# Where the identity, ones and minus-one tiles lie in SBUF, in a fused attention, mixture and gating kernel

## The chip, the cores and the metric

The kernel runs on one core of one Trainium2 chip. The metric is device time in microseconds (us) of one execution; lower is better. The number compared is the median of the runs.

## The reference, cut to what matters

```python
def reference(q, k, v, moe..., moe2...):
    attn = softmax(q k^T / 8 - slope_h * |i - j|, causal, window 128) @ v   # 4 x 8 heads x 576 x 64
    x = attn as [4, 576, 512]
    xn = (x - mean) / sqrt(var + 1e-6) * g_ln
    x = x + relu(xn @ w_ch1) @ w_ch2                                       # 512 -> 2048 -> 512
    h = gelu(x @ w_in); u, v = halves of h                                  # 512 -> 1024
    v = w_sg @ layernorm(v) * g + b_sg
    return x + (u * v) @ w_out
```

The weights arrive as 64-bit floats in pairs of 32-bit words, and every large product is made of three: high times high, low times high and high times low, in the 32-bit matmul type that takes one pass.

## The kernel before

Phase 1 (`phase1`) computes the attention and the first feed-forward layer together. Phase 2 (`Phase2`) computes the gated layer. The feed-forward layer is cut into nine groups of 256 tokens (`g` 0 to 8) and eight slices of the hidden width (`j` 0 to 7); a step of `m1` (line 835) or `m2` (line 846) is two halves of 12 matmuls each. Each matmul loads a stationary block of 128 x 128 from the weight tiles and streams a moving block of 128 x 256 past it. In the profile the moving operand's name stands first behind the arrow and the stationary one's second.

Between these steps a list scheduler (`Sched`, `Op`), whose clock is made of durations written by hand, puts the attention's pieces and the norm's pieces on TensorE. For this case four of them matter, since they are what interrupts the stream of steps:

- the transposes, line 606: `pe.transpose(..., e.t, ident)`. The probabilities are stationary, the identity tile is the moving operand. They are the last piece of every attention burst (score products, line 466, value products, line 650, then two or four transposes), and the next feed-forward matmul follows them;
- the token sums for the mean, line 703: the moving operand is the tile of sums, the ones tile is stationary;
- the sums of squares, line 751: the squares are stationary, one column of ones is moving;
- the broadcast of the reciprocal roots, line 761: the root is stationary, the identity tile is moving.

The tile of minus one is used twice only: for the first two pieces of weights (`NLO = 2`) the low half is made on TensorE (lines 368 and 369), as identity times the weight minus the rounded weight.

The tiles of constants lie in one pool at the bottom of SBUF (`body`, pool `cst`): identity, minus and ones of 512 bytes a partition each, then two small ones. In the built program they start at the bytes 1152, 1664 and 2176 of a partition, which is 128 mod 256 for all three. Everything that is allocated on the left behind them follows from 2752, which is 192 mod 256: `hh`, `hl`, `xh` and `xl` of groups 1 to 8 (the moving operands of the steps) start at 192 mod 256, the weight tiles `w1` and `w2` at 0 mod 256. The `xh` and `xl` of group 0 come from the pool `ap2` on the other side, at 224 mod 256. The tiles of probabilities (`t`) are at 224 mod 256 as well. In phase 2 all tiles are allocated from the right.

The reciprocal roots (`rstd`) lie in a ring of three buffers of 1024 bytes. A tile of zeros for the first, warming matmuls is the first tile that this ring hands out; the roots of groups 0, 1, 2 and so on follow.

Of the kernel before, what the change touches and what calls it, by code (L numbers as in the profile page):

```python
# [7 lines left out]
F32 = mybir.dt.float32  # L8
F32R = mybir.dt.float32r
U8 = mybir.dt.uint8  # L10
I32 = mybir.dt.int32
ACTF = mybir.ActivationFunctionType
# [220 lines left out]
def phase1(tc, nc, a, x2d, cst, p2):  # L233

    sync, act, dve, pool, pe = nc.sync, nc.scalar, nc.vector, nc.gpsimd, nc.tensor
    ident, minus, ones, g1, mh, far = cst
    sched = Sched()

    hp = tc.alloc_tile_pool(name="hp", bufs=2)
# [1 line left out]
    cp = tc.alloc_tile_pool(name="cp", bufs=2)  # L241
    np_ = tc.alloc_tile_pool(name="np", bufs=1)
# [21 lines left out]
    P = {}  # L264
# [11 lines left out]
    def by(o):  # L276

        return {"DVE": dve, "POOL": pool}[o.eng]
# [25 lines left out]
    start, first = {}, {}  # L304
# [14 lines left out]
    def place(n):  # L319

        if n < 24:
            return n // 8, n % 8, slice(0, 512)
        m = n - 24
        z, c0 = (m % 4, m // 4) if m < 8 else (m // 2, m % 2)
        return 3, z, slice(256 * c0, 256 * c0 + 256)
# [14 lines left out]
    def weights(n):  # L340
        q, z, c = place(n)
        w = c.stop - c.start
        late = n >= 24
        st, sc = ("st", NS) if late else ("big", NB), ("sc", NC) if late else ("sc0", 3)
        pri = (WPRI[n] if n < 24 else need[n] - WBACK) + n / 100
        yield Op("SP", 500, WEARLY.get(n, pri), need=["split"] if late else [], slots=[st + (("b3", n),)],
                 token=("wl", n), size=1024 * w)
        p = P["st"] if late else big
        s = p.tile([128, w], I64, tag="st", name="st", bufs=st[1])
        sync.dma_start(out=s, in_=(a["w1"][q, z] if z < 4 else a["w2"][q, z - 4])[:, c])  # L350
        yield Op("ACT", 90 + .93 * w, pri, need=[("wl", n)], slots=[sc + (("w", n),)])
        j = Split64(nc, p, sc[1], s)
        j.first()
        yield Op("DVE", 75 + .51 * w, pri, port=True)
        j.bits(0)
        yield Op("DVE", 75 + .51 * w, pri, port=True)
        j.bits(1)
        yield Op("DVE", 64 + 1.05 * w, pri, port=True)
        j.bits(2)
        yield Op("DVE", 64 + 1.05 * w, pri, token=("b3", n), port=True)  # L360
        j.bits(3)
        yield Op("ACT", 110 + .82 * w, pri, need=["quarter"] if late else [])
        h, l = ((w1 if z < 4 else w2)[q][y][:, z % 4, c] for y in range(2))
        act.activation(out=h, in_=j.x, func=ACTF.Copy)
        if n < NLO:
            yield Op("PE", 1080, pri, need=["cst"], slots=[("h", 2, ("w", n))])
            ps = ps_h.tile([128, 2, 256], F32, tag="h", name="ps_w").rearrange("p a b -> p (a b)")
            pe.matmul(ps, ident, j.x, start=True, stop=False)
            pe.matmul(ps, minus, h, start=False, stop=True)
            yield Op("ACT", 490, pri, token=("w", n))  # L370
            act.activation(out=l, in_=ps, func=ACTF.Copy)
            return
        o = Op(None, 0, pri, token=("w", n), alt=[("POOL", 150 + 2.15 * w, 0), ("DVE", 64 + 1.05 * w, DVEX, 1)])
        yield o
        by(o).tensor_tensor(out=l, in0=j.x, in1=h.bitcast(F32), op=ALU.subtract)
# [300 lines left out]
    xhl, rstd = {}, {}  # L676

    def ln_tile(name):
        return np_.tile([128, 2, 256], F32, tag="ls", name=name, bufs=2)
# [170 lines left out]
    def constants():  # L850
        yield Op("SP", 500, CSTP, token="cst0", size=6 * 2 ** 15, slots=[("ls", 2, "al2")])
        t = ln_tile("cst").rearrange("p a b -> p (a b)").bitcast(BF16)[:, 0:768].rearrange("p (n c) -> p n c", n=6)
        sync.dma_start(out=t, in_=a["cst"].rearrange("p (n c) -> p n c", n=6))
        for z in sms:
            pool.memset(z, 1e-9)
        dve.memset(both, 0.0)
        sched.free["DVE"] = 2300
        yield Op("DVE", 320, -1000, need=["cst0"], token="msk")
        dve.tensor_copy(mask[:, 0:2], t[:, 3:5])
        dve.tensor_scalar(mask[:, 2], t[:, 3], -1.0, 1.0, ALU.mult, ALU.add)  # L860
        yield Op("ACT", 550, -1000, need=["cst0"], token="cst")
        act.activation(out=ident, in_=t[:, 0], func=ACTF.Copy)
        act.activation(out=minus, in_=t[:, 0], func=ACTF.Copy, scale=-1.0)
        for x0 in range(0, 8, 2):
            yield Op("DVE", 270, -1000, need=["cst0"], token="al" if x0 == 6 else None)
            for x in (x0, x0 + 1):
                dve.tensor_scalar(dist[:, x], t[:, 1], 2.0 ** (2 - x), None, ALU.mult)
        yield Op("DVE", 270, -62, token="unf")
        dve.tensor_copy(munf[:, 0], t[:, 5])
        dve.tensor_scalar(munf[:, 1], t[:, 5], -1.0, 1.0, ALU.mult, ALU.add)  # L870
        yield Op("SP", 500, -960, size=2 ** 11)
        sync.dma_start(out=g1, in_=a["g1"])
        for x in range(8, 12):
            yield Op("ACT", 200, -30)
            act.activation(out=dist[:, x], in_=t[:, 2], func=ACTF.Copy, scale=2.0 ** (2 - 4 * ((x - 8) // 2) - x % 2))
        yield Op(None, 0, 0, token="al2")
# [35 lines left out]
    for gen in ([warm(), constants()] + [load_wide(slice(x, y), t) for x, y, t in LW]  # L912
                + [moe(), open_split(), last_quarter(), end_attention()]
                + [weights(n) for n in range(40)] + [norm(g) for g in range(G)]
                + [load(s) for s in runs if not s.wide] + [scores(s) for s in runs] + [burst(s) for s in runs if s.n >= KB] + [unit(e) for e in units]):
        sched.spawn(gen)
# [372 lines left out]
def body(tc, nc, a):  # L1289
    sync, act, dve, pool, pe = nc.sync, nc.scalar, nc.vector, nc.gpsimd, nc.tensor  # L1290
    dp = tc.alloc_tile_pool(name="dp", bufs=1, space=DRAM)
    x2d = [dp.tile([128, 4, 256], F32, name="x2d%d" % g) for g in range(G)]
    with tc.manual_schedule(), tc.tile_pool(name="cst", bufs=1) as cp:
        ident = cp.tile([128, 128], F32, name="ident")
        minus = cp.tile([128, 128], F32R, name="minus")
        ones = cp.tile([128, 128], F32, name="ones")
        g1 = cp.tile([128, 4], F32, name="g1")
        mh = cp.tile([128, 2], F32, name="mh")
        mh, far = mh[:, 0:1], mh[:, 1:2]
        pool.memset(mh, -0.5)  # L1300
        pool.memset(far, NEG)
        pool.memset(ones, 1.0 / DM)
        p2 = Phase2(tc, nc, a, x2d, mh)
        phase1(tc, nc, a, x2d, (ident, minus, ones, g1, mh, far), p2)


def wsT(w):
# [45 lines left out]
```

## Time and profile before

| what | value |
|---|---|
| median of 3 runs | 738.98 us (738.39 to 739.26) |
| profiled execution, its own time | 738.73 us |
| its span, first to last instruction | 737.0 us |
| TensorE busy with matmuls | 720.1 us, 98% of the span |
| VectorE, ScalarE, GpSimd busy | 460.3, 309.1 and 249.2 us |
| mean granted clock of TensorE | 0.993 |

The profile gives busy times by engine and by line, the chain of work that ended last, followed back from the end, and for a stretch of time the busy time and the granted clock. Busy time of matmuls counts overlapping instructions once; so a busy TensorE says nothing of how densely the matmuls follow each other. That is read from the chain: a piece of it that holds 24 matmuls of one line gives, divided by 24, the time from one start to the next (the pitch).

### The profile page before, as it was taken

To read this page: it belongs to the slowest core of one execution; us is meant where nothing else is said; L and a number is where in the kernel's file an instruction comes from. 1 tells how busy PE (TensorE), PEld (TensorE's weight loads), DVE (VectorE), ACT (ScalarE), POOL (GpSimd) and SP (SyncE) were. 2 spreads that over 40 slices of the span, in tenths; PEclk is the share of its full clock that TensorE was granted. 3 is DMA by queue.
4 is the path that set the end of the run, shared out by engine and by line. 5 is a ranking of instruction groups with operands and counts; after the bars stand their busy time and mean duration, and the time that the engine had idled before them with its cause. 6 is when DMAs were issued, how large, how long until landed. Compare 5 with 4: busy or idle time off the path is not lost.

```text
span 737.0 us, 16770 instructions
## 1 busy us (share of the span) xinstructions
PE 720.1 (98%) x6714; PEld 691.0 (94%) x6714; DVE 460.3 (62%) x1200; ACT 309.1 (42%) x795; POOL 249.2 (34%) x296
## 2 busy tenths in 40 slices
PE   6889999999999999999999999999999999999997
PEld 3569999999999999999999999999999999999997
DVE  6999989899572643644543537636676647647632
ACT  5887664554342422522423524323454233344410
POOL 1445250333421321411313324124747307326320
PEclk8999999999999999999999999999999999999999
DMA  8564532023221110111112323403330150160002
GB/s 307 161 213 131 174 118 72 28 93 95 66 98 29 56 51 24 48 59 58 27 49 59 84 85 141 146 29 123 103 116 1 49 159 1 60 198 1 1 33 97
DMA packets 51629, 63.48 MB, mean 86 GB/s; under 512 B 10336, under 2 KB 38880, under 8 KB 51552
## 3 DMA queue, kind: packets, MB, share of 16 engines
q1 hardware_dynamic: 51552, 62.41, 26.5%
q8 instruction: 53, 0.87, 0.5%
q14 instruction: 24, 0.20, 0.1%
HBM read 52.96 MB, written 9.44 MB: 85 GB/s over the span
## 4 chain that ended last, share of the span: by engine, by line
PE 83%; DVE 7%; ACT 5%; issue 2%; POOL 1%; DMA 1%; SPq 0%; DVEq 0%; ACTq 0%
PE ps_h L835 24%; PE acc L846 24%; PE ps_s L1196 8%; PE ps_o L1223 7%; PE ps_v L1100 5%; PE ps_u L1180 5%; PE s L466 2%; PE tps L606 1%; PE o L650 1%; ACT t L517 1%; PE o L606 1%; DVE sc L94 1%; DMA bb<-in_bsg 1%; PE tps L650 1%; DVE sc L97 1%
## 5 line engine op out<-in xcount | busy, mean ns | idle before, releaser
L776 DVE SCALAR_TENSOR_TENSOR hl<-ps_h,hh 128x512 fp32r<-128x512 f32 x72 | 49.7, 690 | 106.6 <-ACT hh L774 105.8
L846 PE MATMUL acc<-hh,w2h 128*128 128x256 f32 x576 | 93.6, 285 | 0.0
L835 PE MATMUL ps_h<-xh,w1h 128*128 128x256 f32 x576 | 92.1, 282 | 0.0
L774 ACT ACTIVATE hh<-ps_h 128x512 fp32r<-128x512 f32 x72 | 42.8, 595 | 116.7 <-PE ps_h L835 116.0
L846 PE MATMUL acc<-hl,w2h 128*128 128x256 f32 x576 | 89.7, 278 | 0.3 <-DVE hl L776 0.3
L835 PE MATMUL ps_h<-xh,w1l 128*128 128x256 f32 x576 | 89.7, 278 | 0.0
L835 PE MATMUL ps_h<-xl,w1h 128*128 128x256 f32 x576 | 89.7, 278 | 0.0
L846 PE MATMUL acc<-hh,w2l 128*128 128x256 f32 x576 | 89.6, 278 | 0.0
L475 POOL TENSOR_SCALAR_AFFINE_SELECT m<-m 128x256 f32<-128x256 f32 (+1 forms) x87 | 41.7, 481 | 136.6 <-ACT m L555 121.8
L835 PEld LDWEIGHTS ps_h<-xh,w1h 128*128 128x128 f32 x576 | 77.2, 189 | 1.3 <-issue 1.2
L846 PEld LDWEIGHTS acc<-hh,w2h 128*128 128x128 f32 x576 | 77.5, 189 | 0.3
L846 PEld LDWEIGHTS acc<-hl,w2h 128*128 128x128 f32 x576 | 76.7, 188 | 0.5 <-DVE hl L776 0.5
L835 PEld LDWEIGHTS ps_h<-xh,w1l 128*128 128x128 f32 x576 | 76.8, 188 | 0.0
L835 PEld LDWEIGHTS ps_h<-xl,w1h 128*128 128x128 f32 x576 | 76.8, 188 | 0.0
L846 PEld LDWEIGHTS acc<-hh,w2l 128*128 128x128 f32 x576 | 76.8, 188 | 0.0
L517 ACT ACTIVATE t<-t,sm 128x128 f32<-128x128 f32 x144 | 56.3, 392 | 28.0 <-DVE sm L511 27.8
L525 POOL TENSOR_TENSOR t<-t,sm 128x256 f32<-128x256 f32 x46 | 28.8, 626 | 72.4 <-DVE sm L521 38.7
L1090 POOL TENSOR_TENSOR gl<-gt,gh 128x576 fp32r<-128x576 f32 x16 | 23.4, 1461 | 49.3 <-ACT gh L1089 46.0
L590 ACT ACTIVATE x<-o 128x256 f32<-128x256 f32 (+1 forms) x40 | 14.3, 358 | 58.3 <-PE o L606 46.1
L85 ACT ACTIVATE sc<-st 128x512 f32<-128x512 f32 (+1 forms) x52 | 30.6, 597 | 16.3 <-DMA st<-in_w 6.6
L1134 ACT ACTIVATE ge<-ge 128x512 f32<-128x512 f32 (+1 forms) x34 | 22.4, 658 | 35.6 <-DVE ge L1133 35.6
L97 DVE SCALAR_TENSOR_TENSOR sc<-st,sc 128x512 int32<-128x512 int32 (+1 forms) x52 | 34.9, 678 | 0.1
(168 smaller groups left out, 1631.9 us busy)
## 6 DMA issues: line engine op xcount, KB each, us to landing
st<-in_w SPq DMA_DIRECT2D x24, 512.0 KB, 4.2
x2d<-x SPq DMA_DIRECT2D x18, 256.0 KB, 2.0
out<-xr SPq DMA_DIRECT2D x15, 288.0 KB, 2.1
st<-in_w SPq DMA_DIRECT2D x16, 256.0 KB, 2.6
st<-in_wi SPq DMA_DIRECT2D x8, 512.0 KB, 3.8
st<-x2d SPq DMA_DIRECT2D x8, 512.0 KB, 4.9
xr<-x2d SPq DMA_DIRECT2D x8, 512.0 KB, 6.6
rq<-in_q SPq DMA_DIRECT2D x28, 128.0 KB, 2.8
```

The costliest lines, as they stand in the source:

```text
L85: self.nc.scalar.activation(out=self.x, in_=self.wh.bitcast(F32), func=ACTF.Abs)
L97: dve.scalar_tensor_tensor(out=xi, in0=self.wl, scalar=29, in1=xi, op0=ALU.logical_shift_right, op1=ALU.bitwise_or)
L475: pool.affine_select(out=out, in_=in_, pattern=pat, compare_op=ALU.is_ge, fill=0.0, base=-1 if up else 0, channel_multiplier=1 if up else -1)
L517: act.activation(out=t[:, h], in_=t[:, h], func=ACTF.Exp, bias=st[:, h:h + 1], scale=-1.0, accum_out=sums[:, h, 0:1])
L774: act.activation(out=h, in_=ps, func=ACTF.Relu)
L776: dve.scalar_tensor_tensor(out=l, in0=ps, scalar=0.0, in1=h.bitcast(F32), op0=ALU.max, op1=ALU.subtract)
L835: pe.matmul(ps[:, half], w[:, kc, f], m[:, kc], start=kc == 0 and x == 0, stop=kc == 3 and x == 2)
L846: pe.matmul(accs[half][:, d], w[:, f, ds], m[:, k], start=fi and d == 0 and k == 0 and x == 0, stop=la and k == 1 and x == 2, skip_group_c ...
L1100: self.nc.tensor.matmul(ps[:, cs], xs[s][:, kc, c0:c0 + 128], self.wv[m][:, kc, cs], start=kc == 0 and x == 0 and z == 0, stop=kc == 3 and ...
L1180: pe.matmul(ps[:, c], wu[s][:, kc, ds], self.x[m][:, kc, c], start=kc == 0 and x == 0, stop=kc == 3 and x == 2)
L1196: pe.matmul(ps[:, c], l, r[:, c], start=n == 0, stop=n == len(mm) - 1)
L1223: pe.matmul(ps[:, c], wo[s][:, kc, ds], gated[b][m][:, kc, c], start=n == 0, stop=n == 11)
```

## The change

The pool of constants begins with an unused tile of 192 bytes (`gap`) and ends with one of 64 bytes (`end`). The identity and ones tiles start at 1344 and 1856, which is 64 mod 256. The tile of minus one leaves the pool; it takes the second buffer of the ring of the roots (`rstd`), whose tiles start at 192 mod 256. The pool is 256 bytes smaller than before, so that what is allocated behind it moves down by 256 bytes and keeps its place mod 256. No instruction of an engine is added or taken away in the source, and the scheduler's durations are the same.

```diff
-    ident, minus, ones, g1, mh, far = cst
+    ident, ones, g1, mh, far = cst
...
             pe.matmul(ps, ident, j.x, start=True, stop=False)
-            pe.matmul(ps, minus, h, start=False, stop=True)
+            pe.matmul(ps, P["minus"], h, start=False, stop=True)
...
         act.activation(out=ident, in_=t[:, 0], func=ACTF.Copy)
-        act.activation(out=minus, in_=t[:, 0], func=ACTF.Copy, scale=-1.0)
+        P["minus"] = np_.tile([128, 256], F32, tag="rstd", name="minus", bufs=3).bitcast(F32R)[:, 0:128]
+        act.activation(out=P["minus"], in_=t[:, 0], func=ACTF.Copy, scale=-1.0)
...
     with tc.manual_schedule(), tc.tile_pool(name="cst", bufs=1) as cp:
+        cp.tile([128, 192], U8, name="gap")
         ident = cp.tile([128, 128], F32, name="ident")
-        minus = cp.tile([128, 128], F32R, name="minus")
         ones = cp.tile([128, 128], F32, name="ones")
         g1 = cp.tile([128, 4], F32, name="g1")
         mh = cp.tile([128, 2], F32, name="mh")
         mh, far = mh[:, 0:1], mh[:, 1:2]
+        cp.tile([128, 64], U8, name="end")
...
-        phase1(tc, nc, a, x2d, (ident, minus, ones, g1, mh, far), p2)
+        phase1(tc, nc, a, x2d, (ident, ones, g1, mh, far), p2)
```

## Rows read from the trace of the kernel before

**Rows 1.** Stretches: window, length, busy us (instructions) by engine, TensorE clock, DMA.
```profile
49.00:52.40 3.40, 3.40 (x29) 2.15 (x19) 3.40 (x9) 2.41 (x8) 0.31 (x2) 0.50 0.60 216
...
60.00:210.00 150.00, 149.32 (x1466) 144.18 (x1466) 129.44 (x356) 82.01 (x225) 53.49 (x68) 1.00 0.31 96
210.00:464.00 254.00, 254.00 (x2689) 248.21 (x2686) 123.28 (x392) 87.88 (x269) 64.76 (x101) 1.00 0.20 60
```

**Rows 2.** Chain that ended last, 244 to 283 us: start, length, what.
```profile
244.58 0.43 PE ps_ln L703 x2
245.01 2.83 PE acc L846 x24
...
255.55 0.34 PE ps_ln L751 x4
255.89 2.93 PE ps_h L835 x24
258.83 0.44 PE ps_r L761 x4
259.27 2.73 PE acc L846 x24
262.00 2.72 PE ps_h L835 x24
...
267.92 0.22 PE tps L606 x2
268.14 1.39 PE acc L846 x12
269.52 2.72 PE ps_h L835 x24
...
280.78 0.22 PE tps L606 x2
281.00 1.42 PE acc L846 x12
282.42 2.83 PE ps_h L835 x24
```

**Rows 3.** The same view, 130 to 141 us: group 0's first products among others.
```profile
130.33 2.74 PE acc L846 x24
133.07 2.83 PE ps_h L835 x24
135.91 2.75 PE acc L846 x24
138.66 2.83 PE ps_h L835 x24
```

**Rows 4.** TensorE's groups by form: line, out<-moving,stationary, shapes, count, busy, mean ns, idle.
```profile
L606 PE MATMUL tps<-ident,t 128*128 128x128 f32 x98 | 21.3, 297 | 6.9 <-POOL t L525 4.8 <-ACT t L481 1.7 <-ACT m L555 0.2
L606 PE MATMUL o<-ident,t 128*128 128x128 f32 x46 | 10.1, 301 | 0.0
L751 PE MATMUL ps_ln<-ones,sq 128*128 128x1 f32 x60 | 7.3, 239 | 0.0
L761 PE MATMUL ps_r<-ident,var 128*128 128x128 f32 x36 | 5.7, 280 | 0.4 <-POOL var L757 0.4
L703 PE MATMUL ps_ln<-sum,ones 128*128 128x256 f32 x16 | 4.9, 385 | 0.0
```

**Rows 5.** Instructions on the minus tile: duration ns min/median/max, first and last start.
```profile
L369 PE MATMUL ps_w<-w1h,minus x2: 794/796/797, 24.2 to 38.5; 128*128 128x512 f32 x2
L863 ACT ACTIVATE minus<-cst x1: 293/293/293, 4.5 to 4.5; 128x128 fp32r<-128x128 bf16 x1
```

**Rows 6.** The same for the tiles of the ring: the roots and the zeros.
```profile
L765 ACT ACTIVATE rstd<-ps_r x9: 356/379/384, 44.3 to 464.3; 128x256 f32<-128x256 f32 x9
...
L884 PE MATMUL warm<-zero x8: 574/634/634, 1.3 to 4.2; 128*128 128x512 bf16 x8
```

**Rows 7.** The chain again, 463 to 491 us, behind the last group's roots.
```profile
463.37 0.44 PE ps_r L761 x4
463.81 2.73 PE ps_h L835 x24
466.54 2.72 PE acc L846 x24
...
488.30 2.72 PE acc L846 x24
```

## The prediction

> **What bounds the kernel now.** I read the stretches by engine first [rows 1]. From 60 to 210 us TensorE is busy for 149.32 of 150 us, from 210 to 464 us for all 254. No other engine is near that; VectorE comes next with 129.44 and 123.28. So between 60 and 464 us time goes only where a matmul follows the one before it later than it could. Busy time can't show that, since matmuls overlap. The chain of work can [rows 2]: a piece of 24 matmuls takes 2.72 us at some places and 2.83 at others, that is 113.3 and 117.9 ns from one start to the next. The shapes, lines and tiles are the same. I call the two pitches fast and slow; they differ by 4.6 ns.
>
> The reader is to see in these rows what a change of pitch follows. Behind the token sums of line 703 the stream goes on slowly (2.83). Behind the squares' sums of line 751 it is slow (2.93 with the first, longer step in it). Behind the root broadcast of line 761 it is fast at once (2.73, 2.72). Behind the transposes of line 606 it is fast once (1.39 for 12, then 2.72) and slow another time (1.42, then 2.83). A pitch, once taken, holds until the next interruption. So the stream seems to lock into one of two rhythms, and the interruption picks which.
>
> I went through this view from 84 to 494 us and took each piece of at least 12 matmuls of lines 835 and 846, by what interrupted last:
>
> - transposes (606): 1210 matmuls fast, 552 slow
> - root broadcast (761): 576 fast, none slow
> - squares' sums (751): none fast, 204 slow
> - token sums (703): 60 fast, 300 slow
>
> The first and last kind of such rows are in [rows 2]. Slow are 1056 in all; at 4.6 ns they cost 4.86 us.
>
> Some slow pieces are slow by their own operands. In [rows 3] two pieces of line 835 take 2.83 us between pieces of line 846 with 2.74 and 2.75, with no interruption between: they are products of group 0, whose moving tiles start at 224 mod 256, where those of all other groups start at 192. There are six such pieces of 24 in the stretch, 144 matmuls, all behind transposes. So the start of an operand mod 256 bears on the pitch in this trace. What is left behind transposes is 552 - 144 = 408 slow matmuls of another cause.
>
> **The change part by part.** *The identity at 64 instead of 128 mod 256.* It is the moving operand of 144 transposes and 36 broadcast passes, and also the stationary one of four passes of line 368. While its last piece streams, the weights of the next step, at 0 mod 256, are loaded. So this move alters what meets at the very place where the pitch is picked. Its own instructions: a pair of transposes takes 0.22 us in the chain, 110 ns each [rows 2]; the trace has identity at one place only, so I bound a change of their pitch by the difference that the trace does show, 4.6 ns either way: (144 + 36) x 4.6 = 0.8 us up or down [rows 4]. I take zero, because a piece of 128 columns at 110 ns is already as long as a full one of 256 at 113, so the moving side isn't what it waits for.
>
> For the pitch behind it: of 1762 matmuls behind transposes 408 could turn fast, 408 x 4.6 = 1.88 us saved; or the 1210 could turn slow, 5.57 us lost; behind broadcasts 576 could turn slow, 2.65 us lost. I take the gain, all 408. The reason is a pattern: in every stream that keeps the fast pitch here, moving tile (192) and weights (0) start an odd number of 64 bytes apart; group 0 (224) breaks it and is slow; identity (128) against the weights (0) breaks it in its own way, by an even number, and its transposes are the interruption with a mixed outcome. At 64 it is odd. The pattern is thin: behind line 761 the same identity at 128 leaves the stream fast every time.
>
> *The ones at 64.* Stationary in the 16 passes of line 703, and one column, moving, in the 60 of line 751 [rows 4]. Behind line 703 the last thing that streams is the sums' tile, whose place stays, while the next weights, whose place stays too, are loaded. Behind 751 the last moving operand is a single column, and the loads before it read the squares. In both the ones' place has little to act on at the moment that counts. Bounds: 504 slow matmuls turn fast, 2.32 us saved; 60 turn slow, 0.28 lost. I take zero.
>
> *Minus in the ring of the roots.* It is read by two passes of line 369, at 24.2 and 38.5 us, and written at 4.5 us [rows 5]. As second tile of the ring it pushes the roots by one buffer: group 0 takes the third, group 1 the zeros' buffer, whose matmuls start by 4.2 us, group 2 that of minus, free after 38.5 us. The first root is written at 44.3 us [rows 6], later ones after it, so no wait on ScalarE's queue ends later than now, and the evacuations that read the roots find them as before. Group 3 reuses group 0's buffer before and after. The scheduler's plan doesn't know either tile's buffer, so the order of work stays. Cost zero; if ScalarE did wait for the readers, it would be behind 38.5 us at worst and still ahead of its first use. The two passes of 0.8 us sit ahead of 40 us, where TensorE still has idle time.
>
> *The rest moves down by 256 bytes.* Mod 256 all stays. Zero, unless the pitch depends on a longer period; no row tests that, and its bounds are those of the pitch above.
>
> **The sum.** Against the profiled execution: 738.73 - 1.88 = 736.85 us. That run lies 0.25 us under the median of 738.98, so 737.1 us for a median. What TensorE gains before 464 us is not lost again: behind 463.37 us it runs on in full pieces of 2.72 us to 491 us [rows 7], and in phase 2 none of the moved tiles is read.
>
> **The rivals.** *Nothing changes.* The pitch behind transposes could be picked by the instant at which the burst ends, not by the identity's place; both outcomes occur in [rows 2] with the identity at one and the same place, which speaks for this. Then one mixed draw replaces another: 739.0 us, with about 1 us either way as stretches of some 90 matmuls (0.4 us) flip.
>
> The Trainium skill ("TensorE: Matmul & The Clock Gate", Part 2, "Step-by-step: what each phase is for") gives the same result by another way: the moving operand and the weights are read through two independent ports, and loading the next weights takes no bandwidth from the running matmul. By that no start of a tile could alter the pitch. The two pitches of equal work [rows 2] and group 0's pieces [rows 3] do not agree with it, so I give it little beyond the first reason.
>
> *Slower: the identity at 64 spoils the broadcast.* Line 761 leaves the stream fast in every case now, with the identity at 128. The place that is given up is thus the only one known to give the fast rhythm reliably. If at 64 the four passes of line 761 leave it slow, 576 matmuls lose 4.6 ns: 2.65 us, 741.6 us. The decisive place is the last of them: from 463.81 us on eleven pieces run at 2.72 without an interruption [rows 7]; if the first piece there takes 2.83, this case holds. With the transposes unchanged it decides alone.
>
> *The ones count after all.* Then the 504 slow matmuls behind lines 703 and 751 become fast too: 737.1 - 2.3 = 734.8 us.
>
> *The granted clock.* Between 49.0 and 52.4 us it is 0.50 [rows 1], behind a stretch in which TensorE was often idle. If the shift in the early work let it stay at 1.0 the gain would be at most half of 3.4 us, 1.7 us. Nothing in the change moves the early work by more than nanoseconds; I fold it into the range.
>
> **How the numbers follow.** Chances: the forecast 0.38 (736.3 to 738.0), nothing changes 0.35 (738.0 to 740.0), the spoiled broadcast or transposes 0.22 (740.0 to 742), the ones too 0.05 (734.5 to 736). A measurement of this kernel can tell about 0.2%, 1.5 us, from no change: that is 737.5 below and 740.5 above. Of the forecast about 0.04 lies above 737.5, which leaves 0.34; the ones' case adds 0.05, and 0.03 of the "nothing" case goes there for a changed clock: faster 0.42. Of the spoiled case 0.20 lies above 740.5, and 0.01 of the "nothing" case: slower 0.21. The rest, 0.37, is within. The range reaches from 734.9, which leaves out the far end of the ones' case, to 741.4, which leaves out the full price of the spoiled one.
>
> **What would show it.** In the chain of the changed kernel: pieces of 24 behind transposes at 2.72, none of 2.83 but group 0's; those behind line 761 still 2.72; those behind lines 703 and 751 still 2.83 and 2.93. The roots' writes begin at 44 us as before, and no piece of ScalarE waits for TensorE there. The forecast is wrong if the share of slow matmuls behind transposes stays near a third, or if pieces behind line 761 rise to 2.83.

## The result: slower by 0.64%

The changed kernel takes 743.35 us (742.82 to 744.26, six runs), the kernel before 738.13 us in runs on the same chip (six runs, 736.01 to 739.26). The ratio is 1.0064, with a 95% interval of 1.0051 to 1.0077. The forecast was 737.1 us and its range ended at 741.4.

The profiled execution takes 743.38 us with a span of 741.7, that is 4.7 us more than the span of before. The same 16770 instructions run. The page of the changed kernel shows the growth in TensorE's busy time (720.1 us before), while VectorE and ScalarE hardly change:

```profile
span 741.7 us, 16770 instructions
...
PE 725.4 (98%) x6714; PEld 695.6 (94%) x6714; DVE 460.8 (62%) x1200; ACT 309.2 (42%) x795; POOL 246.1 (33%) x296
```

The chain of work of the changed kernel, over the part that answers to [rows 2] (start, length, what):

```profile
246.76 0.43 PE ps_ln L703 x2
247.19 2.83 PE acc L846 x24
...
257.73 0.34 PE ps_ln L751 x4
258.07 2.93 PE ps_h L835 x24
261.00 0.44 PE ps_r L761 x4
261.45 2.83 PE acc L846 x24
264.27 2.83 PE ps_h L835 x24
...
270.35 0.22 PE tps L606 x2
270.57 1.42 PE acc L846 x12
271.98 2.83 PE ps_h L835 x24
274.81 2.83 PE acc L846 x24
```

The pieces have the same shapes and the interruptions the same length as before (0.43, 0.34, 0.44, 0.22). What changed is the pitch behind them. Behind the first transposes 24 matmuls took 2.72 us before and take 2.83 now, and behind the root broadcast 2.73 and 2.72 became 2.83. Not every root broadcast is spoiled: two of the six still leave the stream at the fast pitch, the last one as in [rows 7]:

```profile
468.18 0.44 PE ps_r L761 x4
468.62 2.74 PE ps_h L835 x24
471.36 2.72 PE acc L846 x24
```

Counted over the chain from 84 to 494 us, as for the prediction (pieces of at least 12 matmuls, fast up to 116 ns a matmul):

| last interruption | before: fast, slow | after: fast, slow |
|---|---|---|
| transposes (606) | 1210, 552 | 288, 1480 |
| root broadcast (761) | 576, 0 | 336, 192 |
| squares' sums (751) | 0, 204 | 0, 204 |
| token sums (703) | 60, 300 | 144, 216 |
| slow in all | 1056 | 2092 |

The slow pitch has 1036 matmuls more. At 4.6 ns each that is 4.77 us, and the span grew by 4.7. The row of the transposes takes in two places at which score or value products ran last (48 fast and 24 slow matmuls in both kernels).

Two other places were named in the prediction. The roots, on ScalarE, begin 0.9 us later than in [rows 6], and none of them waits for the reader of minus. The granted clock between 49.0 and 52.4 us is now 1.00, but it is 0.50 from 38.0 to 41.4 instead; the stretch of 3.4 us moved and its length stayed, and the mean is 0.993 in both profiles.

```profile
L765 ACT ACTIVATE rstd<-ps_r x9: 360/378/384, 45.2 to 469.1; 128x256 f32<-128x256 f32 x9
```

```profile
38.00:41.40 3.40, 3.40 (x21) 1.59 (x19) 2.24 (x9) 2.78 (x10) 1.21 (x3) 0.50 0.94 358
49.00:52.40 3.40, 3.40 (x41) 2.52 (x41) 3.40 (x14) 2.92 (x11) 1.40 (x3) 1.00 0.53 164
```

### The profile page after: what moved, and what is told of

The parts are those of the page before. It is cut to its first block, busy times and chain, and to the rows that moved or that the text cites. A ratio compares the mean times of both kernels' runs of the same rounds, so it can differ in the third digit from the quotient of the medians.

```text
span 741.7 us, 16770 instructions
## 1 busy us (share of the span) xinstructions
PE 725.4 (98%) x6714; PEld 695.6 (94%) x6714; DVE 460.8 (62%) x1200; ACT 309.2 (42%) x795; POOL 246.1 (33%) x296
## 4 chain that ended last, share of the span: by engine, by line
PE 83%; DVE 9%; ACT 3%; POOL 1%; DMA 1%; issue 1%; DVEq 0%; SPq 0%; ACTq 0%
PE acc L846 24%; PE ps_h L835 24%; PE ps_s L1197 8%; PE ps_o L1224 7%; PE ps_v L1101 5%; PE ps_u L1181 5%; PE s L466 2%; PE o L650 1%; PE tps L606 1%; DVE sc L94 1%; PE o L606 1%; DVE sc L97 1%; PE tps L650 1%; DMA bb<-in_bsg 1%; ACT t L517 1%
## 5 line engine op out<-in xcount | busy, mean ns | idle before, releaser
L1091 POOL TENSOR_TENSOR gl<-gt,gh 128x576 fp32r<-128x576 f32 x16 | 23.4, 1461 | 49.3 <-ACT gh L1090 46.0
```

## The experiments

Theory: the place of the identity tile mod 256, against the place of the weights that are loaded while it streams last, picks the pitch of the step that follows. Rivals: the ring of the roots or the shift by 256 bytes makes the loss; the ones make it; the place acts through the whole burst and not through its last piece; it is the identity's own place, not a distance. A rival that none of the runs tells apart from the theory is the distance from the identity to the moving tiles of the next step: these and the weights lie in the same place to each other in all kernels, but for group 0's.

All experiments start from the changed kernel. The pool's unused tiles are set so that the tiles behind it keep their places mod 256, but for one experiment. The table gives times, ratios to the kernel before (measured again beside each batch of runs, medians 738.93 to 739.14 us) and the counts made as above; the texts stand below it.

| kernel | identity, ones mod 256 | us, median | ratio, 95% interval | 606: fast, slow | 761 | 703 | slow in all |
|---|---|---|---|---|---|---|---|
| e1_minus_only | 128, 128 | 738.55 | 0.9992 (0.9982 to 1.0003) | 1253, 528 | 569, 0 | 60, 300 | 1032 |
| e2_ident64 | 64, 128 | 745.14 | 1.0088 (1.0073 to 1.0103) | 264, 1506 | 120, 404 | 60, 300 | 2414 |
| e3_ones64 | 128, 64 | 738.03 | 0.9978 (0.9966 to 0.9991) | 1288, 492 | 576, 0 | 264, 96 | 792 |
| e4_ident192 | 192, 128 | 742.53 | 1.0048 (1.0035 to 1.0061) | 324, 1465 | 548, 0 | 60, 300 | 1969 |
| f1_ident0 | 0, 64 | 742.95 | 1.0049 (1.0034 to 1.0064) | 372, 1422 | 543, 0 | 84, 276 | 1902 |
| f2_ident160 | 160, 64 | 741.79 | 1.0031 (1.0019 to 1.0043) | 348, 1432 | 550, 0 | 144, 216 | 1852 |
| g1_shift64 | 192, 128; weights at 64 | 736.19 | 0.9958 (0.9944 to 0.9973) | 1461, 324 | 589, 0 | 300, 60 | 588 |

Behind line 751 it is 0 fast and 204 slow in each of them.

**Minus alone moved.**

```diff
-        cp.tile([128, 192], U8, name="gap")
...
-        cp.tile([128, 64], U8, name="end")
+        cp.tile([128, 256], U8, name="end")
```

> Identity and ones stay at 128 mod 256, the tile of minus one is in the ring of the roots and everything behind the pool lies 256 bytes lower. If the place of the identity mod 256 makes the loss, this is the kernel before: 737 to 739 us, and of the matmuls behind the transposes some 30% at the slow pitch (117.9 ns). If the ring or the shift by 256 bytes makes it, it is 742 to 744 us with over 80% slow behind the transposes.

Measured: 738.55 us, the kernel before within its interval, with 528 of 1781 matmuls slow behind the transposes. The ring and the shift by 256 bytes cost nothing. That part of the prediction held.

**The identity alone at 64.**

```diff
         ident = cp.tile([128, 128], F32, name="ident")
+        cp.tile([128, 64], U8, name="mid")
         ones = cp.tile([128, 128], F32, name="ones")
...
-        cp.tile([128, 64], U8, name="end")
```

> Identity at 64, ones at 128 mod 256, minus in the ring. If the identity alone makes the loss: 742 to 744.5 us, over 80% of the matmuls behind the transposes slow. If the ones share in it: about half, 740 to 741 us.

Measured: 745.14 us, more than the whole change and over the expected range. The identity makes the loss alone; with the ones at 64 as well, the changed kernel has 322 fewer slow matmuls (2092 against 2414). Between this kernel and the one before it in the table lie 6.6 us of median, from where a tile of 512 bytes starts, with the same instructions. The chain shows it behind the root broadcast and behind the transposes; first minus alone, then the identity at 64:

```profile
259.91 0.44 PE ps_r L761 x4
260.35 2.73 PE acc L846 x24
263.09 2.72 PE ps_h L835 x24
...
269.00 0.22 PE tps L606 x2
269.22 1.39 PE acc L846 x12
270.61 2.72 PE ps_h L835 x24
```

```profile
261.15 0.44 PE ps_r L761 x4
261.59 2.83 PE acc L846 x24
264.42 2.83 PE ps_h L835 x24
...
270.50 0.22 PE tps L606 x2
270.71 1.42 PE acc L846 x12
272.13 2.83 PE ps_h L835 x24
```

**The ones alone at 64.**

```diff
-        cp.tile([128, 192], U8, name="gap")
         ident = cp.tile([128, 128], F32, name="ident")
+        cp.tile([128, 192], U8, name="mid")
         ones = cp.tile([128, 128], F32, name="ones")
```

> Identity at 128, ones at 64 mod 256, minus in the ring. If the ones' place has nothing to act on, as the prediction had it: 737 to 739 us and the counts behind lines 703 and 751 nearly all slow, as before. If it bears on the pitch behind lines 703 and 751: up to 2.3 us less than with the ones at 128.

Measured: 738.03 us and 0.9978, with 264 fast behind line 703 where 60 were. The ones do bear on the pitch behind the token sums, in which they are stationary, and at 64 not on that behind the squares' sums. Their place doesn't decide alone: with the same ones at 64 and the identity at 0 or 160, the table has only 84 and 144 fast there. So the change held a small gain and a large loss. The gain is read from the counts; in time this kernel and minus alone can't be told apart (0.9966 to 0.9991 and 0.9982 to 1.0003). The chain behind the token sums, where minus alone has 2.83 at the same place:

```profile
245.71 0.43 PE ps_ln L703 x2
246.15 2.75 PE acc L846 x24
248.89 2.72 PE ps_h L835 x24
```

**The identity at 192, at 0 and at 160.**

```diff
-        cp.tile([128, 192], U8, name="gap")
+        cp.tile([128, 64], U8, name="gap")
         ident = cp.tile([128, 128], F32, name="ident")
+        cp.tile([128, 192], U8, name="mid")
         ones = cp.tile([128, 128], F32, name="ones")
...
-        cp.tile([128, 64], U8, name="end")
```

That is the identity at 192. For 0 the two tiles have 128 and 64 bytes, for 160 they have 32 and 160, and the end tile of 64 stays.

> Identity at 192, where the moving tiles of the steps lie, ones at 128 mod 256. The prediction's rule of an odd number of 64 bytes to the weights (at 0) has 192 fall with 64: then 742 to 744 us. If each place picks by itself, or if 192 is good because the steps' own moving tiles start there: 736 to 738 us with under 15% slow behind the transposes.

> Identity at 0, ones at 64 mod 256. With the identity at 64 and 192 some 80% of the matmuls behind the transposes were slow, at 128 some 28%. If an even number of 64 bytes between the identity and the weights (at 0) is what helps, 0 is like 128: under 35% slow, 736 to 739 us. If 128 alone helps (half a turn away): over 70% slow, 741 to 744 us.

> Identity at 160, ones at 64 mod 256: no longer on a multiple of 64. If the start in steps of 64 is what counts, 160 reads across the steps like group 0's tiles at 224 and gives a mixed or slow outcome: 739 to 743 us. If the rule were the distance to the probabilities' tile (at 224), 160 would be 192 away from it, the distance that the steps themselves have: under 20% slow, 735 to 737 us.

Measured: behind the transposes 82% of the matmuls are slow at 192, 79% at 0 and 80% at 160; at 128 it was 28 to 31%, at 64 between 84 and 85%. Only 128 is good, with the weights at 0. An odd number of 64 bytes is slow both times (64, 192), an even one once slow and once good (0, 128); a multiple of 64 doesn't decide, nor a distance of 192 to the probabilities' tile. The root broadcast is another matter: behind it the stream is fast at 0, 128, 160 and 192 in these kernels, and mixed at 64 (404 of 524 matmuls slow with the ones at 128, 192 of 528 in the changed kernel). The identity at 192 and at 0, behind transposes:

```profile
269.48 1.42 PE acc L846 x12
270.90 2.83 PE ps_h L835 x24
```

```profile
270.18 0.22 PE tps L606 x2
270.39 1.42 PE acc L846 x12
271.81 2.83 PE ps_h L835 x24
```

**Another piece last.** Two kernels with the transposes ahead of the value products, in the bursts that `burst` issues, one with the identity at 64 and one at 128 (ones at 64 in both).

```diff
-        values(runs[n - 1])
         for e in s.units:
             transposed(e)
+        values(runs[n - 1])
```

> The changed kernel with the transposes of each burst from run 13 on ahead of its value products, so that the identity at 64 is no longer the last that streams ahead of a step. If the last moving operand picks the pitch: the slow share behind these bursts is that of the twin with the identity at 128, whatever it is, and both kernels are within 1 us of each other but for line 761 (up to 0.9 us). If the identity counts through the whole burst: 3 to 5 us over the twin.

> The twin: identity at 128, ones at 64, the transposes ahead of the value products. Under the theory of the last moving operand it equals the one with the identity at 64 within 1 us; otherwise it is 3 to 5 us less, near 738 us.

Measured: 746.71 us (1.0102, 1.0087 to 1.0117) and 746.11 us (1.0094, 1.0079 to 1.0109). With another piece last the two places of the identity are within 0.6 us, where they were over 5 us apart with the transposes last (743.35 and 738.03). The count as above gives 576 slow of 1785 matmuls behind these bursts with the identity at 64 and 666 of 1776 at 128, but 372 of each stand in the first piece behind the value products, which opens with longer steps and so counts as slow whatever the pitch behind them. In the pieces after the first, 1185 matmuls are fast and 132 slow with the identity at 64, 1086 and 222 at 128. So the identity's place counts where its transposes run last, and not through the burst as a whole. Behind the root broadcast it is 444 fast and 60 slow at 64, 492 and none at 128.

Both kernels are slower than the kernel before although their streams are mostly fast, since the burst itself takes longer. In the starts of the matmuls in the traces, the 18 bursts that hold score products, value products and transposes take 45.7 us in both kernels, each from the last step's matmul ahead to the second behind, and 39.4 in the kernel with the ones alone at 64, with the same 728 matmuls in them. Part of that stands in the first 12 matmuls behind them. Twin with the identity at 64, then at 128:

```profile
270.63 0.06 PE tps L650 x2
270.68 1.57 PE acc L846 x12
272.25 2.72 PE ps_h L835 x24
```

```profile
270.73 1.58 PE acc L846 x12
272.31 2.72 PE ps_h L835 x24
```

**A distance or a place?** The kernel with the identity at 192, and everything behind the pool 64 bytes higher: the weights at 64 and the steps' moving tiles at 0 mod 256.

```diff
         mh, far = mh[:, 0:1], mh[:, 1:2]
+        cp.tile([128, 64], U8, name="end")
```

> Identity at 192 and ones at 128 mod 256, as in the run before with the identity at 192, and one more tile of 64 bytes at the pool's end, so that all tiles behind it move up by 64: the weights start at 64, the steps' moving tiles at 0 mod 256. If the distance from the identity to the next weights picks the pitch (192 - 64 = 128, as in the kernel before): 25 to 40% of the matmuls behind the transposes are slow, 737 to 740 us. If the identity's own start picks it: over 70% slow, 741 to 744 us, as with the identity at 192 and the weights at 0.

Measured: 736.19 us, ratio 0.9958; 324 of 1785 slow behind the transposes, where the identity at 192 with the weights at 0 had 1465 of 1789. So it is a distance that picks, and not the identity's own start: that start and that of the ones are the same in both kernels, and the tiles behind the pool moved. Which distance isn't shown. In the good kernels the identity lies 128 bytes from the next weights, and also 64 below the next moving tiles (128 and 192, here 192 and 0); the weights and the moving tiles moved together. The distance of the ones changed as well: they lie 64 from the weights, as with the ones alone at 64, and behind the token sums 300 matmuls are fast. That kernel is thus the nearer twin (738.03 us, ratio 0.9978, 792 slow in all). The 204 slow matmuls fewer, and a share of 18% where 25 to 40% were expected, stay unexplained; the probabilities and group 0's tiles stayed at 224 and so lie otherwise to the weights. It has the lowest median of all kernels here and is faster than both kernels of this case. Behind the two transposes that are mixed in [rows 2], all is fast:

```profile
267.52 0.22 PE tps L606 x2
267.74 1.38 PE acc L846 x12
269.12 2.72 PE ps_h L835 x24
...
280.36 0.22 PE tps L606 x2
280.58 1.38 PE acc L846 x12
281.96 2.72 PE ps_h L835 x24
```

**Group 0's tiles, and other places of the ones.** The identity at 128, the ones at 64, and `xh` and `xl` of group 0 at 192 like those of the other groups; then the same with the ones at 0 and at 192.

```diff
+        if not g:
+            ap2.tile([128, 224], U8, name="pad0", bufs=1)
         xh = cpool.tile([128, 4, 256], F32R, tag="xh", name="xh", bufs=bufs)
         xl = cpool.tile([128, 4, 256], F32R, tag="xl", name="xl", bufs=bufs)
+        if not g:
+            ap2.tile([128, 32], U8, name="pad1", bufs=1)
```

> Identity at 128, ones at 64 mod 256, minus in the ring, and the tiles xh and xl of group 0 at 192 instead of 224 mod 256. If the start of the moving tile makes group 0's matmuls slow, some 170 of them turn to the pitch of the others: 0.5 to 0.9 us less than with the ones alone at 64, that is 736 to 738 us, ratio about 0.997. If something else of group 0 makes them slow (its place in the order, the pool on the other side): no change from the run with the ones alone.

> As before with group 0's tiles at 192, and the ones at 0 mod 256. With the ones at 128 some 83% of the matmuls behind the token sums (line 703) were slow, at 64 some 27%. If the ones' start, as the stationary tile, picks that pitch, 0 gives a share of its own, between 0 and 300 slow ones, worth up to 1.4 us; if the pitch before the interruption decides, the share follows the pieces ahead of it and no start is better than another.

> The same with the ones at 192 mod 256, the start of the sums' tile that streams past them. Same reading: a share of its own behind line 703, worth up to 1.4 us between all slow and all fast; behind line 751 all 204 slow, as with every start of the ones so far.

Measured: 737.32 us (0.9971, 0.9960 to 0.9982), 740.04 us (1.0016, 1.0006 to 1.0025) and 738.27 us (0.9985, 0.9974 to 0.9996). Group 0's own pieces (here line 839, for 835) lose their own slow pitch, as the first of the three shows at the place of [rows 3]:

```profile
130.63 2.75 PE acc L850 x24
133.37 2.72 PE ps_h L839 x24
136.09 2.72 PE acc L850 x24
138.81 2.72 PE ps_h L839 x24
```

But the sum moves little: 768 slow matmuls in all against 792, since other stretches behind transposes turned slow (468 behind them, where 492 had held group 0's 144). One reason can be seen behind the transposes at 167 to 168 us: with group 0's tiles at 224 the step of line 846 behind group 0's first slow piece is fast again (2.75 us), and with them at 192 the slow pitch goes on through all six pieces (2.82 or 2.83). The times of the two kernels, 0.9971 and 0.9978, can't be told apart. The ones at 192 give 60 fast and 300 slow behind line 703, as at 128; the ones at 0 give 96 and 264.

The ones at 0 also do something that nothing here had announced: 192 fast and 374 slow behind the root broadcast, in which they take no part, 688 slow behind the transposes, and 24 fast and 180 slow behind the squares' sums, in which one column of them is the moving operand. The chain shows how they reach the broadcast:

```profile
459.15 0.34 PE ps_ln L755 x4
459.49 1.47 PE ps_h L839 x12
460.96 2.72 PE acc L850 x24
463.68 0.44 PE ps_r L765 x4
464.13 2.83 PE ps_h L839 x24
466.96 2.83 PE acc L850 x24
```

Here the squares' sums (line 755, for 751) leave the stream fast, and the broadcast (line 765, for 761) turns it slow. Counted from the starts of the matmuls, this happens three times. At the other three broadcasts of this kernel the stream ahead is slow and the one behind fast, and so it is at all 60 broadcasts with a step behind them in the ten kernels with the identity at 0, 128, 160 or 192 and the ones elsewhere. So the pitch behind the broadcast depends on the pitch ahead of it: an interruption doesn't pick alone, and a stretch hands something of its rhythm on.

## Why the prediction was wrong

**What held.** The reading of the chain: two pitches of equal work, which change at interruptions and at group 0's pieces. Over the twelve kernels with the transposes last, the median time follows the number of slow matmuls in a straight line of 4.5 ns a matmul (the prediction's 4.6; the kernel before taken at 739.04 us), from 588 and 736.19 us to 2414 and 745.14, with no kernel over 0.7 us from it. The cost of nothing for the ring and for the shift by 256 bytes held (minus alone, 0.9992).

**The step that failed** is "I take the gain, all 408". It rested on a pattern of odd and even numbers of 64 bytes that had one identity tile at one place behind it. The runs give the places their outcomes: of the five starts only 128, with the weights at 0, is good, and that is where the identity had been. The bound on the other side, 1210 matmuls turning slow, is what happened to 922 of them (1210 to 288). At 4.6 ns that is 4.24 us; the root broadcasts add 192 matmuls, 0.88 us, and the token sums take back 84, 0.39 us. The sum is 4.73 us, and the span grew by 4.7.

**The rival on the slow side** had the wrong interruption. It priced the root broadcast (2.65 us if all went slow) and named the transposes only in the chance. What it put in a sentence, that the place given up is the one with the known good rhythm, was the right argument and belonged to the transposes as well: at 128 they left 69% of the stream fast (1210 of 1762). A mixed outcome was read as a bad one. And that the broadcast is fast "in every case" rested on six places that all had a slow stretch ahead; the ones at 0 show it slow three times behind a fast one, with the identity still at 128.

**The range** ended at 741.4 because it took in the price of the broadcast alone. The price of the transposes, 5.57 us, stood in the text as a bound and never reached the range.

**The ones**: "little to act on at the moment that counts" was wrong for line 703. With the ones alone at 64 some 204 more matmuls are fast behind it, about 0.9 us, and the time fell by 0.1 to 0.3% against the kernel before. For line 751 it was right at 64, 128 and 192, and wrong at 0.

**Nothing changes** fell with it: the share of slow matmuls behind the transposes went from 31% to 84%, which is no other draw of the same kind. The page that stood beside this rival, the Trainium skill's "TensorE: Matmul & The Clock Gate" (Part 2, "Step-by-step: what each phase is for"), has the streamed operand and the weights read through two independent ports, so that loading takes nothing from the running matmul. The prediction drew from it that no start could alter the pitch; the 6.6 us between two kernels that differ in starts alone speak against that, and the measurement decides. What meets inside TensorE or on the way to it, no run shows.

**What stays open.** Why 128 is good for the transposes, and whether it is the distance to the next weights or to the next moving tiles. Why at 128 some bursts still leave the stream slow. Why the root broadcast, with the same identity tile streaming last, leaves the stream slow at 64 at four of six places in the changed kernel, at five with the ones at 128, and at one of six with the transposes ahead of the value products. No run here looks inside a weight load, and I tried no other distance than these five.

## What to carry to other kernels

When TensorE is busy all the time, divide the length of a chain piece by its matmuls, and look at whether equal pieces have more than one pitch; if so, sort the pieces by what interrupted last, and by the pitch ahead of the interruption, before moving anything. Where a tile's start mod 256 may decide, one trace with the tile at one place prices both directions and says nothing of the sign: put the full price of both into the range, and try the places in turn, each alone. An outcome that is mostly good is a place to keep until another has been measured.

## What the runs showed of the hardware

- A stream of equal matmuls of 256 columns settles at 113.3 or 117.9 ns from start to start at a granted clock of 1.00 (the 2.4 GHz level), and keeps the pitch until something else runs in between or steps with a moving tile at 224 mod 256 come (24 matmuls took 2.83 us ahead of one such piece and 2.75 behind it).
- Which one it is depends on where the last streamed operand starts, mod 256, against the tiles of the steps behind it (weights and moving tiles moved together here): with the identity 128 from the weights 18 to 39% of the matmuls behind the transposes are slow, at 0, 64, 160 and 192 between 79 and 85%.
- It also depends on the pitch ahead: with the identity at 128 the root broadcast turned a slow stream fast at every place, and a fast one slow at the three places where one came (2.72 us for 24 ahead, 2.83 behind).
- A moving tile at 224 mod 256 had a slow pitch of its own (2.83 us for 24), which went to 2.72 with the tile at 192.
- Kernels with the same matmuls in the same order, apart from such starts, spread over 9 us (736.19 to 745.14).
